# Holding the unshifted term of a VectorE batch until all four tiles are there, in a list-scheduled attention kernel

## The chip, the cores and the metric

One Trainium2 chip, one core, one launch. Times are device microseconds (us) of an execution. Most figures are medians of three to nine executions; a span is that of one profiled execution, from its first instruction to its last, and is some 1.7 us shorter than the time of the same execution. A ratio is the mean time of one kernel's fast runs over that of the other's in the same rounds on the same chip, so it is not quite the ratio of the medians quoted.

## The reference, cut to what matters

Four blocks in a row on x of shape 1 x 2048 x 512: attention, linear attention, attention, linear attention. The attention block has 32 heads of 16 columns that share one K and one V.

```python
def _A_ref(x, wq, wk, wv, wo):           # H = 32, Dh = 16, S = 2048
    q = (x @ wq).reshape(B, S, H, Dh).transpose(0, 2, 1, 3)
    k, v = x @ wk, x @ wv
    p = softmax(einsum("bhqd,bkd->bhqk", q, k) * Dh ** -0.5)
    o = einsum("bhqk,bkd->bhqd", p, v)
    return o.transpose(0, 2, 1, 3).reshape(B, S, H * Dh) @ wo
x = x + _A_ref(_layernorm(x), ...)       # layer 0
x = x + _B_ref(_layernorm(x), ...)       # linear attention, no softmax
x = x + _A_ref(_layernorm(x), ...)       # layer 1
x = x + _B_ref(_layernorm(x), ...)
```

The two softmaxes over 32 x 2048 x 2048 scores are most of the work.

## The kernel before

The program is not written in order. A list scheduler runs while the kernel is built: it has an operation's readiness, a modelled duration and a priority for each engine, and fixes the order of every engine's instructions. What the chip then does is that order, with semaphores.

The scores of both layers are cut into 4096 tiles of 128 x 512. ScalarE exponentiates two or three tiles in one instruction. The other tiles go to VectorE, four to a batch: an integer multiply and add writes a bit pattern that reads as a rough power of two (the unshifted term, P1), three copies with shifted exponents are added to it, and TensorE sums the four terms with four weighted copies of V. So a VectorE tile needs four value matmuls, a ScalarE tile one.

```python
# dstep: one score tile for VectorE; four make a batch
o = add(PE, PASS, lambda e: self.smm(e, [p], db), ..., name="sD", pk=("S", ...))
o = add(DV, tdv(512), lambda e: e.tensor_scalar(out=PTD[:, hp.idx, i * 512:(i + 1) * 512], in0=bank(db),
        scalar1=SCALE * LOG2E * 128.0, scalar2=TOFF, op0=ALU.mult, op1=ALU.add), ..., name="P1")
c["p1"].append(o)
# ... (cut)
# dpass: the terms of a batch; dep[i] is tile i's P1 for r == 0, the shift's one instruction otherwise
for r in range(NTERM):
    dep, src = c["p1"], hp
    split = r == NTERM - 1 and m == 4 and self.npx < NPX and bool(p_ptd.free)
    if split:                       # last term: four pieces on GpSimd
        dep, src = self.pieces(c, m, r, done)
    elif r:                         # one 128x2048 shift on VectorE
        dep, src = self.shift(c, m, r, done)
    for i, p in enumerate(c["pos"]):
        pv = self.add_pv(p, ..., src, dep[0 if r and not split else i], r, 1)
# ... (cut)
# add_pv: a value matmul uses one of TensorE's four column groups
return e.matmul(ps[32 * c:32 * c + 32, 7 * 512:8 * 512], lhsT=Vaug[:, kt, r, :], rhs=..., ...)
# ... (cut)
# Sched._try: a port-sharing VectorE operation does not start while GpSimd is at work
if e == DV and o.port and self.tfree[PO] > self.now + 1e-9 or e == PO and self.dport > self.now + 1e-9:
    continue
```

Some thirty constants steer the scheduler (priorities, how far VectorE may run ahead, how many value matmuls are worth a change of mode). A table, PLAN, changes them every 6 us of modelled time.

The softmax here doesn't subtract the row's maximum and nothing guards it: scores larger than these inputs give would overflow.

## Time and profile before

| | |
|---|---|
| time | 1495.28 us median of 3 (1494.65 to 1497.23) |
| span of the profiled execution | 1497.1 us (its time was 1498.80 us) |
| ScalarE tiles | 2954, in 598 instructions of three and 580 of two |
| VectorE tiles | 1142 |
| ScalarE, sum of service times (see the prediction) | 1420 us |

The groups and the busy line of this profile stand in the prediction. In a group, the figure after the bar is the busy time and the mean ns of one instruction, then the idle time of that engine just before such instructions and what ended it.

### The profile page before, as it was taken

The numbers are of one execution on the slowest core, as the hardware profiler recorded it, in microseconds if no ns is written. First come the engines' busy times: TensorE is split into PE (matmuls) and PEld (weight loads), VectorE is DVE, ScalarE is ACT, GpSimd is POOL, SyncE is SP. The second block draws the span as 40 slices with busy tenths as digits, with TensorE's granted clock in tenths as the row PEclk, the third lists the DMA queues.
The fourth block names the chain that finished last, engine by engine and source line by source line (L and its number), as shares of the span: only waits on it lengthen the run. The fifth ranks groups of instructions, "written<-read, shape, count | busy, mean of one in ns | idle before, by whom it ended". The sixth has DMA issues, their size and how long they took to land.

```text
span 1497.1 us, 38261 instructions
## 1 busy us (share of the span) xinstructions
PE 1459.2 (97%) x16245; PEld 492.0 (33%) x16255; DVE 1376.5 (92%) x2433; ACT 1444.9 (97%) x1426; POOL 853.2 (57%) x1360
## 2 busy tenths in 40 slices
PE   7999999999999999999899999999999999999998
PEld 4322333322333333333442333333333232333334
DVE  7999998999988999899798999989999899989987
ACT  7999999999999999999698999999999999999996
POOL 3556656565563655565544556566565456565654
PEclk9999999999999999999998999999999999999999
DMA  3000000000000000000000000000000000000001
GB/s 118 26 9 5 9 12 5 5 5 4 14 6 7 5 5 17 9 8 9 2 1 5 5 9 8 9 5 5 5 5 15 6 5 5 9 16 8 6 9 57
DMA packets 46251, 17.71 MB, mean 12 GB/s; under 512 B 39936, under 2 KB 45568, under 8 KB 46080
## 3 DMA queue, kind: packets, MB, share of 16 engines
q1 hardware_dynamic: 46080, 15.27, 4.3%
q8 instruction: 127, 2.08, 0.6%
q14 instruction: 44, 0.36, 0.1%
HBM read 5.28 MB, written 2.10 MB: 5 GB/s over the span
## 4 chain that ended last, share of the span: by engine, by line
PE 58%; ACT 23%; DVE 19%; issue 1%; POOL 0%; DMA 0%; SPq 0%; ACTq 0%
PE ps_all L1072 24%; PE ps_all L1035 23%; ACT PTA L1192 20%; DVE PTD L1252 10%; PE ps_all L768 7%; DVE PTD L1323 5%; PE ps_all L772 2%; PE ps_all L1093 2%; DVE Eo L1084 1%; DVE stats L840 1%; ACT e_buf L1576 1%; ACT e_buf L1439 1%; ACT e_buf L1577 1%; DVE e_buf L1446 0%; DVE x_sb L1431 0%
## 5 line engine op out<-in xcount | busy, mean ns | idle before, releaser
L1192 ACT ACTIVATE PTA<-ps_all 128x1536 bf16<-128x1536 f32 (+1 forms) x1178 | 1357.8, 1292 | 18.7 <-PE ps_all L1035 15.0
L1313 POOL TENSOR_SCALAR PTD<-PTD 128x512 uint16<-128x512 uint16 x1124 | 683.2, 618 | 489.2 <-DVE PTD L1323 317.6
L1252 DVE TENSOR_SCALAR PTD<-ps_all 128x512 uint16<-128x512 f32 x1142 | 751.1, 680 | 69.9 <-PE ps_all L1035 65.4
L1035 PE MATMUL ps_all<-QT,Kr 32*128 32x512 bf16 x4141 | 658.6, 385 | 9.9 <-ACT PTA L1192 3.6
L1072 PE MATMUL ps_all<-PTD,Vaug 128*32 128x512 bf16 x4568 | 616.2, 386 | 5.8 <-DVE Eo L1084 5.2
L1072 PE MATMUL ps_all<-PTA,Vaug 128*32 128x512 bf16 x2954 | 533.8, 387 | 0.2
L1323 DVE TENSOR_SCALAR PTD<-PTD 128x2048 uint16<-128x2048 uint16 x577 | 403.6, 711 | 2.2
L1035 PEld LDWEIGHTS ps_all<-QT,Kr 32*128 32x128 bf16 x4141 | 169.1, 91 | 493.0 <-ACT PTA L1192 220.1
L1072 PEld LDWEIGHTS ps_all<-PTD,Vaug 128*32 128x32 bf16 x4568 | 158.6, 94 | 218.1 <-issue 141.5
L1072 PEld LDWEIGHTS ps_all<-PTA,Vaug 128*32 128x32 bf16 x2954 | 131.8, 94 | 145.8 <-issue 114.2
L768 PE MATMUL ps_all<-wqkv_sb,xnT 128*32 128x512 bf16 x960 | 72.5, 382 | 0.1
L1448 POOL TENSOR_SCALAR e_buf<-e_buf 128x512 f32<-128x512 f32 x60 | 36.8, 613 | 43.1 <-ACT e_buf L1439 23.9
L1446 DVE TENSOR_SCALAR e_buf<-ps_all 128x512 f32<-128x512 f32 x60 | 40.9, 685 | 14.3 <-ACT e_buf L1439 14.2
L1439 ACT ACTIVATE e_buf<-ps_all 128x512 f32<-128x512 f32 x64 | 41.7, 655 | 9.7 <-PE ps_all L772 6.5
L1450 POOL TENSOR_TENSOR pqT<-e_buf 128x512 bf16<-128x512 f32 x30 | 38.0, 1268 | 11.8 <-DVE PTD L1323 8.0
L1450 POOL TENSOR_TENSOR pk_tok<-e_buf 128x512 bf16<-128x512 f32 x30 | 38.1, 1272 | 10.5 <-DVE PTD L1323 9.4
L1084 DVE COPY Eo<-ps_all 128x512 f32<-128x512 f32 x62 | 42.3, 682 | 1.5 <-PE ps_all L1072 1.3
L840 DVE BATCH_NORM_STATS2 stats<-x_sb 128x6 f32<-128x512 bf16 x64 | 42.9, 678 | 0.5 <-DMA x_sb<-in_A_x_dram 0.2
L1093 PE MATMUL ps_all<-identf,Eo 128*128 128x128 f32 x256 | 42.4, 289 | 0.0
L768 PE MATMUL ps_all<-wo_sb,OT 128*32 128x512 bf16 x480 | 37.7, 382 | 0.0
L1578 POOL TENSOR_TENSOR pqT<-pqT,e_buf 128x512 bf16<-128x512 bf16 x20 | 23.2, 1164 | 25.1 <-ACT e_buf L1577 6.5
L929 POOL TENSOR_SCALAR Vaug<-Vaug 128x32 bf16<-128x32 bf16 x48 | 14.9, 311 | 32.1 <-DVE Vaug L925 15.5
(102 smaller groups left out, 686.2 us busy)
## 6 DMA issues: line engine op xcount, KB each, us to landing
out_dram<-x_sb SPq DMA_DIRECT2D x16, 128.0 KB, 1.7
OT<-Osb SPq DMA_TRANSPOSE x120, 2.4
xnT<-xn_buf SPq DMA_TRANSPOSE x120, 2.3
wqkv_sb<-in_B_wqkv_dram SPq DMA_DIRECT2D x4, 384.0 KB, 3.1
x_sb<-in_A_x_dram SPq DMA_DIRECT2D x3, 256.0 KB, 3.4
x_sb<-in_A_x_dram SPq DMA_DIRECT2D x1, 768.0 KB, 7.9
wq_sb<-in_A_wq_dram SPq DMA_DIRECT2D x1, 512.0 KB, 6.4
x_sb<-in_A_x_dram SPq DMA_DIRECT2D x1, 512.0 KB, 8.7
```

The source lines that it names most:

```text
L768: i = e.matmul(out[32 * c:32 * c + 32], lhsT=lhsT[:, 32 * c:32 * c + 32], rhs=rhs, start=start, stop=stop, skip_group_check=True)
L840: add(DV, tdv(512), lambda e: e.bn_stats(stats[:, t, 0:6], x_sb[:, t, :]), reads=[("x", t)], writes=[("st", t)], prio=prio, name="bn")
L1035: x = e.matmul(bank(b0 + k), lhsT=Kr[r, m, kt * P:(kt + 1) * P], rhs=QT[r, self.units[u][0] % 2, gs, q0:q0 + n], start=True, stop=True)
L1072: return e.matmul(ps[32 * c:32 * c + 32, 7 * 512:8 * 512], lhsT=Vaug[:, kt, r, :], rhs=src() if callable(src) else src, start=opened[0], s ...
L1084: return (e.copy if oe.eng == AC else e.tensor_copy)(Eo[:, he.idx, :], bank(7))
L1093: i = e.transpose(bank(ht.idx, P, qs * P), Eo[:, he.idx, qs * P:(qs + 1) * P], identf[:])
L1192: oe = add(AC, tac(m * 512), lambda e: e.activation(PTA[:, hp.idx, 0:m * 512], bank(SETS[s][0], m * 512), ACTF.Exp, scale=SCALE), deps=[o] ...
L1252: o = add(DV, tdv(512), lambda e: e.tensor_scalar(out=PTD[:, hp.idx, i * 512:(i + 1) * 512], in0=bank(db), scalar1=SCALE * LOG2E * 128.0, ...
L1313: return e.tensor_scalar(out=PTD[:, ht.idx, i * 512:(i + 1) * 512], in0=PTD[:, hp.idx, i * 512:(i + 1) * 512], scalar1=float(SHIFT[r]), sc ...
L1323: return e.tensor_scalar(out=PTD[:, ht.idx, 0:512 * m], in0=PTD[:, hp.idx, 0:512 * m], scalar1=float(SHIFT[r]), op0=ALU.add, **kw)
L1439: o1 = add(AC, tac(512), lambda e: e.activation(e_buf[:, he.idx, :], bank(h.idx), ACTF.Exp), deps=[o], uses=[h], acq=[he] if fast else [he ...
L1450: add(PO, PHS, lambda e: e.tensor_tensor(out=dst, in0=sh(e_buf[:, hr.idx, :]), in1=sh(e_buf[:, he.idx, :]), op=ALU.add), deps=[o2, o3], us ...
```

## The change

Its intent: VectorE's tiles become ready one after the other, and a value matmul that goes alone uses one of four column groups, so the unshifted term is to wait until its four matmuls can go side by side. With it come a rule for the port that VectorE and GpSimd share, and a new table.

```diff
+PBL = 0.04
+R0 = 1
 PLAN = (
-    (0.0, {... 'NT0': 3, 'DMIN': 1, ... 'MF': 0.285, ... 'PX': 2.788, ...}),
+    (0.0, {... 'NT0': 5, 'DMIN': 2, ... 'MF': 0.413, ... 'PX': 0.523, ...}),
     ... (nearly every row is another)
-            if e == DV and o.port and self.tfree[PO] > self.now + 1e-9 or ...:
+            if e == DV and o.port and self.tfree[PO] > 0.0 and self.tfree[PO] + PBL > self.now + 1e-9 or ...:
                 continue
     ... (cut)
+        if e == PO:
+            self.at(end + PBL, None)
     ... (cut)
-    pv = self.add_pv(p, ..., src, dep[0 if r and not split else i], r, 1)
+    pv = self.add_pv(p, ..., src, c["p1"][-1] if R0 and not r else dep[0 if r and not split else i], r, 1)
```

## The prediction

> **What bounds the kernel now.** I read the page from the top: busy times, slices, chain, groups.
>
> ```profile
> PE 1459.2 (97%) x16245; PEld 492.0 (33%) x16255; DVE 1376.5 (92%) x2433; ACT 1444.9 (97%) x1426; POOL 853.2 (57%) x1360
> ...
> PE 58%; ACT 23%; DVE 19%; issue 1%; POOL 0%; DMA 0%; SPq 0%; ACTq 0%
> ...
> L1192 ACT ACTIVATE PTA<-ps_all 128x1536 bf16<-128x1536 f32 (+1 forms) x1178 | 1357.8, 1292 | 18.7 <-PE ps_all L1035 15.0
> L1313 POOL TENSOR_SCALAR PTD<-PTD 128x512 uint16<-128x512 uint16 x1124 | 683.2, 618 | 489.2 <-DVE PTD L1323 317.6
> L1252 DVE TENSOR_SCALAR PTD<-ps_all 128x512 uint16<-128x512 f32 x1142 | 751.1, 680 | 69.9 <-PE ps_all L1035 65.4
> L1035 PE MATMUL ps_all<-QT,Kr 32*128 32x512 bf16 x4141 | 658.6, 385 | 9.9 <-ACT PTA L1192 3.6
> L1072 PE MATMUL ps_all<-PTD,Vaug 128*32 128x512 bf16 x4568 | 616.2, 386 | 5.8 <-DVE Eo L1084 5.2
> ```
>
> Three engines look nearly full, so busy shares do not name the bound. The first and third groups show how the work is dealt: 4096 score tiles of 512 columns, of which ScalarE exponentiates 2954 in 1178 instructions (598 of three tiles, 580 of two) and VectorE 1142, one each. Every VectorE tile gets four terms, so 4 x 1142 = 4568 value matmuls.
>
> I then looked at single instructions, in time order, in a steady stretch.
>
> ```profile
> 699.07 12.32 ACT L1192 ACTIVATE PTA<-ps_all 128x1024 bf16<-128x1024 f32 x11
> ...
> 705.26 0.39 PE L1072 MATMUL ps_all<-PTD,Vaug 128*32 128x512 bf16 x4
> ...
> 706.33 0.10 PEld L1072 LDWEIGHTS ps_all<-PTD,Vaug 128*32 128x32 bf16 x2 [0.23 <-issue]
> ...
> 706.56 0.59 PE L1072 MATMUL ps_all<-PTD,Vaug 128*32 128x512 bf16 x5
> ```
>
> ScalarE runs eleven exponentials (both sizes; the row prints the first one's) with no gap. TensorE's four value matmuls take 0.39 us together and five take 0.59 us: one round of four column groups costs some 0.2 us more, and 0.39 is mostly the pipe's length. TensorE's 97% is therefore not its throughput; ScalarE's nearly is.
>
> To size that I used the records' start times. A three-tile exponential is followed by the next start after 1331 ns (median), a two-tile one after 904 ns, though they last 1482 and 1067. Taking for every ScalarE form the tenth percentile of its start-to-start times as its service gives 1420 us of service, of which 598 x 1.331 + 580 x 0.904 = 1320 us is the exponentials. From first to last instruction ScalarE spans 1490 us, so it loses about 70 us; 7 us of the span lie outside. The same sum for VectorE gives 1305 us of service and 188 us lost. **ScalarE bounds the kernel**, VectorE has slack. ScalarE's losses by stretch: about 11 us in the first 40 us of feeding and layer norm, some 14 us at the layer change (700 to 800), 7 us near the end (1440 to 1480), and in the steady part 16 us (100 to 680) and 22 us (800 to 1400).
>
> Of the last, one piece stands out; the windows of it:
>
> ```profile
> 812.00:815.00 3.00, 2.52 (x20) 0.45 (x16) 2.49 (x4) 1.59 (x3) 1.13 (x2) 0.67 0.01 3
> 815.00:818.00 3.00, 3.00 (x20) 1.09 (x20) 1.82 (x4) 1.70 (x2) 0.03 (x1) 0.50 0.00 0
> 818.00:822.00 4.00, 4.00 (x27) 0.51 (x23) 2.65 (x5) 2.48 (x2) 1.80 (x3) 0.50 0.13 25
> 822.00:826.00 4.00, 4.00 (x31) 0.82 (x28) 2.51 (x4) 2.48 (x2) 1.88 (x4) 0.50 0.05 8
> ```
>
> The columns are busy time on TensorE, weight load, VectorE, ScalarE and GpSimd, then the granted clock. From 813.0 us TensorE ran 13.7 us at half clock, ScalarE fell to 1.6 to 2.5 us in each window, and its longest steady waits stand here: 1.57, 1.70, 0.60, 1.04 and 1.47 us, together 6.4 us. It is the only dip in the run.
>
> **What the Trainium skill says.** "Perfetto Trace Analysis", section "Identifying the Most-Contended Engine", says that TensorE's matmul busy share is no good measure and that occupancy is fair for Scalar and Vector; the trace agrees, as the rounds above show. The same page, "DVE / Act Engine Instruction", says that a record ends at the write's acknowledgement while the next may begin earlier; the trace agrees: 1482 ns long, 1331 ns apart. "TensorEngine Tiling (Array Packing)", section "Key Properties", says that a change of tiling mode drains TensorE; the 0.23 us ahead of the first weight load after such a change fits. "SBUF — State Buffer", section "SBUF: two separate sides", says that a VectorE two-port operation and a GpSimd one exclude each other for a whole instruction. The trace fits: GpSimd's pieces waited 317.6 us for VectorE's shifts (L1323); and of these shifts a quarter are followed within 601 ns, but the median by 647 ns.
>
> **The change part by part.** There are three, and the program is laid out at build by a list scheduler, so I compared the instruction order of both builds.
>
> 1. The unshifted term's four value matmuls become ready with the last of the four tiles, not each with its own. It removes no instruction. Counted in the built orders: before, the 1142 unshifted matmuls stand in 784 unbroken runs, 546 of a single one and 33 of four; after, 1139 stand in 679 runs, 412 single and 64 of four. So quartets get commoner, but other value matmuls of equal priority still come between. In rounds of 512 columns (in each stretch of one mode, the fullest tile group under in-order issue) the value-type stretches take 2744 before and 2811 after, score stretches 1776 and 1729, full-array work 438 and 425: 4958 against 4965 in all. Without the filler matmuls (four narrow or one wide make a round; 39 rounds before, 36 after) it is 4919 against 4929. Stretches of one mode, so drains, go from 2483 to 2515: 32 x 0.23 = 7 us more. **TensorE is given no less to do**, and it is not the bound.
>
> 2. The scheduler now counts 40 ns after a GpSimd operation before it lets VectorE start a port-sharing one. The roughly 50 ns (647 less 597) on half of 574 shifts is 14 us of VectorE time that the old schedule did not know of. Knowing it cannot remove much, but keeps the order nearer to what the chip does. It lies on VectorE, beside ScalarE's work; its worth is a few us of fewer late tiles.
>
> 3. The table of scheduler constants is new in nearly all of its 6 us steps. By the order it leaves the work almost alone. ScalarE: one more three-tile exponential (+1.33 us), three more key evictions (3 x 0.36), one more projected-matrix and one more value copy, one query copy less, one more mask product: together +2.9 us. VectorE: 3 tiles less (3 x 0.60), 6 shifts less (6 x 0.60), ten query products moved to GpSimd (10 x 0.65): about -12 us. GpSimd: +12 pieces x 0.60, +10 products x 1.13, four phi passes less: about +11 us at 57% busy. Neither is on the path.
>
> Sum for the bound: 1420 + 3 = 1423 us of ScalarE service. What can move is the 70 us of loss. Startup, layer change and end (some 32 us) keep their instructions: 53 rows after the last exponential instead of 51, and 66 between two exponentials at the layer change instead of 63. The steady loss without the dip is 38 - 6 = 32 us; I choose that the better-tracked schedule takes a fifth of it, -6 us. The dip I give an even chance of being gone: -3 us. In all 1495.3 + 3 - 6 - 3 = **1489 us**.
>
> **The rivals.**
> - Packing was the hidden bound: full quartets end ScalarE's waits for score matmuls. For it: those waits are all on TensorE (L1035). Against it: rounds are not fewer. At best the steady 32 us go: near 1465 us.
> - A new wait in place of the old: TensorE works in order, and a late last tile now holds all four matmuls and everything behind them, while the raw buffer stays held. For it: VectorE's start-to-start times scatter. Against it: the shifted terms waited for that last tile anyway, and VectorE got only 3 tiles fewer. It would cost 5 to 15 us: 1500 to 1510 us.
> - The clock: no dip 1489 less 3, two dips 1489 plus 10. Filler matmuls change from 44 narrow and 28 wide to 84 and 15, so the duty around the layer change is another; I can't tell which way.
> - Nothing: the loss is the same and only the work differs, 1498 us.
>
> **Range and chances.** The first case at half effect gives 1477, the second at its low end 1501. Faster by 2% is 1465 us and needs nearly all steady loss gone; slower by 2% is 1525 us, ten times the added work. I give 4%, 93% and 3%.
>
> **What would show it.** Right: ScalarE's exponentials stay at 1331 and 904 ns apart, its service is near 1423 us, its wait for L1035 falls from 15.0 us by a few us, L1252's wait for L1035 stays in the tens, and no group changes its mean. Shift starts at 647 ns should become fewer. The prediction is wrong if the wait of TensorE's weight loads for L1252 or GpSimd grows and ScalarE's wait with it (second rival), if ScalarE's steady loss falls under 15 us (first), or if the clock row shows another number of dips.

## The result, and the profile after

The changed kernel took 1498.66 us (median of 4, 1498.50 to 1498.71) beside 1496.26 us (4 runs): ratio 1.0017, interval 1.0000 to 1.0034. Five more rounds (after_again, below) gave 1.0015, interval 1.0002 to 1.0029. It is the same by the 2% measure, and a trace slower, where 0.4% faster had been forecast.

The busy line, the chain by engine and the groups of the changed kernel, to be held against those in the prediction (L1192 is now L1196, L1313 L1317, L1252 L1256, L1035 L1039, L1072 L1076):

```profile
PE 1458.3 (97%) x16282; PEld 491.5 (33%) x16282; DVE 1362.2 (91%) x2413; ACT 1446.9 (97%) x1432; POOL 862.9 (58%) x1374
...
PE 53%; ACT 38%; DVE 7%; POOL 1%; issue 1%; DMA 0%; POOLq 0%
...
L1196 ACT ACTIVATE PTA<-ps_all 128x1024 bf16<-128x1024 f32 (+1 forms) x1179 | 1356.8, 1297 | 13.9 <-PE ps_all L1039 10.5
L1317 POOL TENSOR_SCALAR PTD<-PTD 128x512 uint16<-128x512 uint16 x1136 | 690.7, 617 | 502.8 <-DVE PTD L1327 341.0
L1256 DVE TENSOR_SCALAR PTD<-ps_all 128x512 uint16<-128x512 f32 x1139 | 752.1, 681 | 75.7 <-PE ps_all L1039 70.4
L1039 PE MATMUL ps_all<-QT,Kr 32*128 32x512 bf16 x4150 | 639.7, 383 | 13.8 <-ACT PTA L1196 8.1
L1076 PE MATMUL ps_all<-PTD,Vaug 128*32 128x512 bf16 x4556 | 622.2, 384 | 3.6 <-DVE Eo L1088 3.0
```

In the lines shown, no count and no mean moved by more than 1.1%. The trace has one spell at half clock, of 3.4 us at 726 us, where the one before had 13.7 us at 813 us. ScalarE's wait for score matmuls seems to have fallen, from 15.0 to 10.5 us, just as forecast; the next section shows that this is the clock and not the change. The busy times of VectorE, ScalarE and TensorE are the old ones within 1.1%.

### The profile page after: what moved, and what is told of

It is laid out like the page before. It is cut to its first block, busy times and chain, and to the rows that moved or that the text cites. A ratio compares the mean times of both kernels' runs of the same rounds, so it can differ in the third digit from the quotient of the medians.

```text
span 1496.8 us, 38319 instructions
## 1 busy us (share of the span) xinstructions
PE 1458.3 (97%) x16282; PEld 491.5 (33%) x16282; DVE 1362.2 (91%) x2413; ACT 1446.9 (97%) x1432; POOL 862.9 (58%) x1374
## 4 chain that ended last, share of the span: by engine, by line
PE 53%; ACT 38%; DVE 7%; POOL 1%; issue 1%; DMA 0%; POOLq 0%
ACT PTA L1196 35%; PE ps_all L1076 22%; PE ps_all L1039 20%; PE ps_all L772 6%; DVE PTD L1256 3%; PE ps_all L776 2%; PE ps_all L1097 2%; DVE PTD L1327 1%; ACT e_buf L1443 1%; DVE stats L844 1%; POOL pqT L1582 1%; ACT e_buf L1580 1%; ACT e_buf L1581 1%; DVE Eo L1088 0%; DVE e_buf L1450 0%
## 5 line engine op out<-in xcount | busy, mean ns | idle before, releaser
L1196 ACT ACTIVATE PTA<-ps_all 128x1024 bf16<-128x1024 f32 (+1 forms) x1179 | 1356.8, 1297 | 13.9 <-PE ps_all L1039 10.5
L1317 POOL TENSOR_SCALAR PTD<-PTD 128x512 uint16<-128x512 uint16 x1136 | 690.7, 617 | 502.8 <-DVE PTD L1327 341.0
L1256 DVE TENSOR_SCALAR PTD<-ps_all 128x512 uint16<-128x512 f32 x1139 | 752.1, 681 | 75.7 <-PE ps_all L1039 70.4
L1039 PE MATMUL ps_all<-QT,Kr 32*128 32x512 bf16 x4150 | 639.7, 383 | 13.8 <-ACT PTA L1196 8.1
L1076 PE MATMUL ps_all<-PTD,Vaug 128*32 128x512 bf16 x4556 | 622.2, 384 | 3.6 <-DVE Eo L1088 3.0
L1076 PE MATMUL ps_all<-PTA,Vaug 128*32 128x512 bf16 x2957 | 543.5, 386 | 0.0
L1327 DVE TENSOR_SCALAR PTD<-PTD 128x2048 uint16<-128x2048 uint16 x571 | 393.7, 703 | 1.6
L1039 PEld LDWEIGHTS ps_all<-QT,Kr 32*128 32x128 bf16 x4150 | 165.0, 91 | 485.8 <-ACT PTA L1196 234.8
L1076 PEld LDWEIGHTS ps_all<-PTD,Vaug 128*32 128x32 bf16 x4556 | 159.1, 94 | 218.3 <-issue 141.9
L1076 PEld LDWEIGHTS ps_all<-PTA,Vaug 128*32 128x32 bf16 x2957 | 134.2, 94 | 147.7 <-issue 106.5
L1582 POOL TENSOR_TENSOR pqT<-pqT,e_buf 128x512 bf16<-128x512 bf16 x30 | 34.3, 1163 | 26.6 <-ACT e_buf L1581 20.3
L776 PE MATMUL ps_all<-Msb,pqT 128*128 128x512 bf16 x128 | 32.5, 379 | 0.9
```

Source lines behind the costliest of these rows:

```text
L776: return e.matmul(out, lhsT=lhsT, rhs=rhs, start=start, stop=stop, skip_group_check=True)
L1039: x = e.matmul(bank(b0 + k), lhsT=Kr[r, m, kt * P:(kt + 1) * P], rhs=QT[r, self.units[u][0] % 2, gs, q0:q0 + n], start=True, stop=True)
L1196: oe = add(AC, tac(m * 512), lambda e: e.activation(PTA[:, hp.idx, 0:m * 512], bank(SETS[s][0], m * 512), ACTF.Exp, scale=SCALE), deps=[o] ...
L1317: return e.tensor_scalar(out=PTD[:, ht.idx, i * 512:(i + 1) * 512], in0=PTD[:, hp.idx, i * 512:(i + 1) * 512], scalar1=float(SHIFT[r]), sc ...
L1327: return e.tensor_scalar(out=PTD[:, ht.idx, 0:512 * m], in0=PTD[:, hp.idx, 0:512 * m], scalar1=float(SHIFT[r]), op0=ALU.add, **kw)
```

## The experiments

Eighteen kernels ran. My theory at the start was that ScalarE alone bounds the kernel, that packing is worth nothing, and that the new table takes a few us of ScalarE's losses. The rivals were that TensorE's packing bounds after all, and that the three parts have large effects that cancel.

A first build tells something before any run: the old table with the wait for four tiles added does not build. The scheduler ends with value matmuls that never became ready. A table belongs to its rule more closely than I had thought. (With both rules the old table does build; that kernel was not run.)

### The same kernels once more

before_again is the text of the changed kernel with all three parts undone; the order of every engine is the kernel before's to the instruction.

```diff
-PBL = 0.04            -R0 = 1            -PLAN = (new table)
+PBL = 0.0             +R0 = 0            +PLAN = (old table)
```

> The changed kernel's text with all three parts undone (no wait for all four tiles, no 40 ns, the old table): the built order equals the kernel before in every instruction, so this is a second look at the kernel before. Theory (the clock spell belongs to the old order): 1494 to 1498 us, and its trace shows the one half-clock spell near 813 us again, of some 14 us. Rival (the spell is chance): no spell or one elsewhere, and a span up to 6 us shorter than 1497 us.

It took 1495.29 us, in a run of four that held one of 1505.96 us at a lower mean clock (0.990). Its trace has a span of 1492.4 us, and no spell at half clock near 813 us, only one of 3.4 us at 1467 us. The rival held. The same windows as in the prediction, of before_again:

```profile
812.00:815.00 3.00, 2.52 (x28) 0.99 (x30) 3.00 (x6) 2.11 (x2) 0.97 (x2) 1.00 0.01 3
815.00:818.00 3.00, 3.00 (x35) 0.66 (x30) 3.00 (x8) 3.00 (x4) 1.16 (x2) 1.00 0.06 11
818.00:822.00 4.00, 4.00 (x48) 1.17 (x46) 4.00 (x7) 4.00 (x5) 2.74 (x6) 1.00 0.13 25
822.00:826.00 4.00, 4.00 (x49) 1.15 (x45) 4.00 (x8) 3.86 (x4) 2.74 (x5) 1.00 0.02 4
```

From 815 us on ScalarE (the fourth busy figure) and VectorE (the third) are full or nearly so here, where they stood idle for a third of the time or more in the trace of before. One and the same order has the spell in one execution and not in the next; with it the span is 4.7 us longer. The first trace was no typical execution: the 38 later executions of the kernel before, on four chips, have medians of 1494.5 to 1495.5 us by chip and round, with single ones up to 1505.94; 36 of them have a mean clock of 0.997 or more, where the traced one had 0.995. ScalarE's wait for score matmuls is 10.2 us in this trace,

```profile
L1196 ACT ACTIVATE PTA<-ps_all 128x1536 bf16<-128x1536 f32 (+1 forms) x1178 | 1357.5, 1295 | 13.8 <-PE ps_all L1039 10.2
```

so there is no fall from 15.0 to 10.5 us where the old order runs without that spell.

after_again is the changed kernel with a blank line added.

> The changed kernel again (a blank line added), five rounds beside the kernel before. Theory (no gain, a little longer round the layer change): 1497 to 1500 us, 1.001 to 1.004 of the kernel before with an interval that leaves out 0.996. Rival (my predicted 0.996 was missed by chance in few runs): ratio under 0.999.

It took 1497.38 us (five runs, 1497.34 to 1498.68) beside 1495.40 us of nine, ratio 1.0015 (1.0002 to 1.0029); no spell in its trace, span 1495.6 us. Its order and before_again's can be compared with little of the clock in the way. I sum ScalarE's services as in the prediction (1331 and 904 ns for the exponentials of both, the tenth percentile of its own start-to-start times for every other form) and call the rest between first and last instruction lost. "Start" is up to 60 us past the first exponential, "change" from 10 us before the last one of layer 0 to 80 us past the first of layer 1, "end" the last 10 us of exponentials and all behind; flat_both, with both rules and no table, comes below.

| us | before_again | after_again | flat_both |
|---|---|---|---|
| span | 1492.4 | 1495.6 | 1555.3 |
| ScalarE's service | 1419.4 | 1420.7 | 1436.9 |
| lost at the start | 7.5 | 6.5 | 8.1 |
| lost in the steady parts | 34.1 | 33.7 | 64.9 |
| lost at the layer change | 15.9 | 17.6 | 23.2 |
| lost at the end | 8.0 | 9.1 | 14.2 |
| outside ScalarE's first and last | 7.4 | 7.9 | 7.8 |
| at half clock | 3.4 | 0.0 | 17.1 |

The steady parts, for which the whole change was made, lose what they lost. The 3.2 us more are 1.3 of service, 1.7 at the layer change, 1.1 at the end, less 1.0 at the start, and some 0.5 outside, within rounding. The 3.4 us at half clock of before_again lie in its end, so the two orders differ there by rather more than 1.1. ScalarE in time order at the layer change, of before_again:

```profile
711.60 1.48 ACT L1196 ACTIVATE PTA<-ps_all 128x1536 bf16<-128x1536 f32 x1
...
717.21 1.09 ACT L1443 ACTIVATE e_buf<-ps_all 128x512 f32<-128x512 f32 x2 [2.83 <-PE ps_all L776]
...
725.02 0.58 ACT L881 COPY xnT<-ps_all 128x512 bf16<-128x512 bf16 x1 [1.43 <-PE ps_all L875]
...
749.52 1.43 ACT L1196 ACTIVATE PTA<-ps_all 128x1536 bf16<-128x1536 f32 x1
```

and of after_again:

```profile
710.00 3.77 ACT L1197 ACTIVATE PTA<-ps_all 128x1536 bf16<-128x1536 f32 x3
...
725.92 0.59 ACT L882 COPY xnT<-ps_all 128x512 bf16<-128x512 bf16 x1 [2.15 <-PE ps_all L876]
...
749.52 1.11 ACT L1581 ACTIVATE e_buf<-ps_all 128x512 f32<-128x512 f32 x2
750.48 1.20 ACT L1582 ACTIVATE e_buf<-e_buf 128x512 f32<-128x512 f32 x2
752.17 1.45 ACT L1197 ACTIVATE PTA<-ps_all 128x1536 bf16<-128x1536 f32 x1 [0.50 <-PE ps_all L1040]
```

Layer 0's exponentials end at 713.1 and 713.8 us, layer 1's begin at 749.5 and 752.2 us: 36.4 us against 38.4 us between them. At 749.5 us, where the old order starts with layer 1, the new one still has two pairs of the linear block's logarithm and exponential to do. So 2 of the 3 us lie in a stretch that the wait for four tiles does not touch; the new table put it so.

The clock can also be taken out of the times. Within one kernel they follow the mean granted clock: the four runs of flat_none (below) took 1548.41 us at 0.999, 1550.70 at 0.997, 1555.49 at 0.993 and 1560.98 at 0.988. One slope fitted to the runs of all eighteen kernels and of the kernel before beside them is 1.29 us for each 0.001, and leaves a scatter of at most 1.4 us (standard deviation) in any of them. Taken to a clock of 1 by this line, which makes them estimates, before_again and the kernel before lie 0.2 us apart, as the same order should, and after_again is 3.9 us slower than the kernel before. (An order may itself draw more or fewer spells; no run here tests that.)

### Which engine holds the time

Three kernels keep the changed kernel's order and take work from one engine. Their outputs are wrong, which doesn't matter for the times. A fourth, thin_both, takes from two.

```diff
 # thin_exp: once a buffer was filled, three-tile exponentials compute 1408 of 1536 columns
-activation(PTA[:, hp.idx, 0:m * 512], bank(SETS[s][0], m * 512), ACTF.Exp, ...)
+activation(PTA[:, hp.idx, 0:w], bank(SETS[s][0], w), ACTF.Exp, ...)          # w = 1408
 # thin_value: all but the first and last value matmuls of an accumulation stream 448 columns
-e.matmul(ps[32 * c:32 * c + 32, 7 * 512:8 * 512], lhsT=..., rhs=src, ...)
+e.matmul(ps[32 * c:32 * c + 32, 7 * 512:7 * 512 + n], lhsT=..., rhs=src[:, 0:n], ...)   # n = 448
 # thin_p1: once a slot was filled, VectorE's P1 computes 460 of 512 columns
-tensor_scalar(out=PTD[:, hp.idx, i * 512:(i + 1) * 512], in0=bank(db), ...)
+tensor_scalar(out=PTD[:, hp.idx, i * 512:i * 512 + w], in0=bank(db, w), ...)            # w = 460
```

> Wrong result on purpose. The changed kernel with its order untouched, but all but the first few three-tile exponentials on ScalarE compute 1408 of 1536 columns: some 594 x 0.107 us = 63 us less ScalarE work. Theory (ScalarE bounds): 1498 less 50 to 63, so 1435 to 1448 us. Rival (TensorE bounds): at most 15 us less.

> Wrong result on purpose. The changed kernel with its order untouched, but all value matmuls except the first and last of an accumulation stream 448 columns instead of 512: rounds fall from 2811 to 2557, some 54 us less TensorE work. Theory (ScalarE bounds): 1490 to 1499 us. Rival (value matmuls and their packing bound): 1445 to 1465 us.

> Wrong result on purpose. The changed kernel with its order untouched, but VectorE's tiles (the eviction that makes the unshifted term) compute 460 of 512 columns once each buffer slot was filled once: some 1090 x 0.054 us = 59 us less VectorE work. Theory (VectorE has slack): 1488 to 1499 us. Rival (VectorE bounds with ScalarE): below 1465 us.

> Wrong result on purpose. The changed kernel, order untouched, with both cuts: three-tile exponentials at 1408 columns and value matmuls at 448. Alone they gave 16 and 9 us. Theory (ScalarE and TensorE are a few us apart, each hides the other's cut): well over the sum, 40 to 60 us less, 1438 to 1458 us. Rival (a third thing, the chain between engines, holds both): 25 us or less, 1473 us or more.

| kernel | work taken away | median us | ratio to before | worth, us |
|---|---|---|---|---|
| thin_exp | 63 us of ScalarE | 1482.96 | 0.9918 | 14.5 |
| thin_value | 54 us of TensorE | 1489.97 | 0.9967 | 7.2 |
| thin_p1 | 59 us of VectorE | 1496.88 | 1.0014 | 0.1 |
| thin_both | 63 of ScalarE and 54 of TensorE | 1466.01 | 0.9807 | 31.1 |

Since the thin kernels and after_again did not run in the same rounds, the worth is taken from the ratios: after_again's 1.0015 less the kernel's, times 1495 us. (The expectation of thin_both counts from 1498.7 us, and so has 16 and 9.) The intervals of the two ratios together leave each worth uncertain by some 3 us; taken to full clock, thin_p1's is 3 us and the others change by less than 2. VectorE's slack came as forecast, and TensorE gave little alone. ScalarE did not behave: less than a quarter of the work taken from it showed up, which is what the rival (TensorE bounds) had expected. My theory of one bound fell here. The chains that ended last, by engine, of thin_exp, thin_value and thin_both:

```profile
PE 70%; DVE 25%; ACT 3%; POOL 1%; issue 0%; DMA 0%; POOLq 0%
```

```profile
ACT 57%; PE 31%; DVE 10%; POOL 1%; issue 1%; DMA 0%; POOLq 0%; SPq 0%
```

```profile
PE 59%; DVE 36%; ACT 3%; POOL 1%; issue 1%; DMA 0%; POOLq 0%; SPq 0%
```

With shorter exponentials ScalarE, which had 38% of the chain in the changed kernel, all but leaves it, and TensorE takes it over. (The chain is one path only: ScalarE's share is 23% in before, 27% in before_again and 38% in after, three kernels of nearly one speed.) The group of the exponentials in thin_exp says the same:

```profile
L1201 ACT ACTIVATE PTA<-ps_all 128x1024 bf16<-128x1024 f32 (+2 forms) x1179 | 1311.8, 1197 | 38.8 <-PE ps_all L1039 30.5
```

Its wait for score matmuls goes from 10.5 to 30.5 us, and its loss by my sum from 67 us (after_again) to 117 us. So my reading is that ScalarE is first, that the work through TensorE stands some 15 us behind, and that the two hide each other's cuts: both together give 31.1 us, more than the 21.7 of the single ones. That is the theory that I put in place of the first, and it is not shown whole: a ScalarE that was plainly first would have left thin_value nothing, and thin_both's 31.1 us lie between the 40 to 60 of the theory and the 25 of its rival. They don't give 54 either. ScalarE still loses 99 us in thin_both, and VectorE has 36% of the chain; a third limit, VectorE or the waits between three engines in a fixed order, is next. Which of the two, no run settles.

For the question at hand this is enough: 254 rounds of value matmuls fewer gave 7 us. The change saves no round at all (2811 against 2744 among value-type stretches), so there is nothing for it to give.

### The two rules without a tuned table

Four kernels use one constant row (the kernel's own default) in place of the table, with neither rule, with one, and with both.

```diff
-PLAN = ( ... some 240 rows ... )
+PLAN = ()            # R0 = 0 or 1, PBL = 0.0 or 0.04
```

> One constant row in place of the table of scheduler constants, neither wait nor 40 ns. Leaves ScalarE 3012 tiles (58 more than the kernel before, 58 x 0.444 = 26 us). Both theories: 1505 to 1530 us. It is the base line for the next three, whose table was tuned for neither rule.

> The constant row with the wait for all four tiles alone. Against the constant row with nothing. Theory (packing is worth nothing: rounds 5108 against 5112): within 6 us of it, from ScalarE's 3018 tiles + 3 us. Rival (filled column groups pay): over 10 us faster than it. Second rival (the later release costs): over 10 us slower.

> The constant row with the 40 ns rule alone. ScalarE gets 3021 tiles, + 4 us against the constant row with nothing. Theory (the rule only makes the schedule truer): within 6 us of it. Rival (it repairs late tiles): over 10 us faster.

> The constant row with both rules. ScalarE gets 3005 tiles, - 3 us. Theory: within 6 us of the constant row with nothing. Rival (the two rules pay only together): over 10 us faster.

They took 1553.10, 1548.44, 1554.23 and 1554.61 us. flat_none is far over its expected 1505 to 1530 us: I had counted only the 26 us of ScalarE tiles. The other three lie within 5 us of it, as expected. One pair can't tell a worth of 5 us from the scatter between two schedules, so I ran two more pairs, with a constant row taken from each table at 120 us.

```diff
-PLAN = ()
+PLAN = ((0.0, {the row that the new (old) table holds at 120 us}),)     # R0 = 0 or 1, PBL = 0.0
```

> One constant row again, now the one that the new table holds at 120 us, without the wait for all four tiles and without the 40 ns. ScalarE keeps 3033 tiles. Base line for the next run; 1520 to 1570 us.

> The same row with the wait for all four tiles alone. Rounds 5069 against 5097, stretches of one mode 2570 against 2624, ScalarE 10 tiles less (- 4 us). Theory (the wait by itself is worth the few us of rounds and drains that it saves, at most 0.5%): 0 to 8 us faster than its base line. Rival (worth nothing): within 2 us. Second rival (filled column groups pay well): over 15 us faster.

> One constant row, the one that the old table holds at 120 us, neither rule. ScalarE keeps 2943 tiles. Base line for the next run; 1500 to 1580 us.

> That row with the wait for all four tiles alone. Rounds 5063 against 5093, stretches 2548 against 2556, ScalarE 6 tiles more (+ 3 us). Theory: 0 to 8 us faster than its base line. Rival (worth nothing): within 2 us or slower. Second rival (filled column groups pay well): over 15 us faster.

| row | without the wait | with it | difference | rounds | stretches of one mode |
|---|---|---|---|---|---|
| the default | 1553.10 | 1548.44 | -4.7 | 5112, 5108 | 2630, 2581 |
| from the new table | 1564.73 | 1565.72 | +1.0 | 5097, 5069 | 2624, 2570 |
| from the old table | 1537.01 | 1534.35 | -2.7 | 5093, 5063 | 2556, 2548 |

The mean is 2 us, the sign changes, and the runs of one kernel spread by up to 12 us (1561.96 to 1574.05 in rowN_none) with their clock (0.995 to 0.987). The second row came as its rival had it, worth nothing, the third as the theory. But the clock was lower with the wait in the second row (mean 0.986 against 0.992); taken to full clock the three differences are -2.2, -7.6 and -5.3 us. A fourth pair, flat_40ns and flat_both, has +0.4 us as measured and +1.2 at full clock. Over the four pairs that is a mean gain of 1.5 us as measured and 3.5 at full clock. The wait may be worth a few us; it is not worth 15. The 40 ns rule made both of its pairs slower, by 1.1 us (flat_none to flat_40ns) and 6.2 us (flat_wait4 to flat_both).

Since the wait alone seldom keeps a quartet together, one more kernel lets the unshifted matmuls go ahead of other value matmuls, which leaves 166 unbroken quartets in the built order where flat_wait4 has 49.

```diff
-prio=2.0 + 1e-4 * u, ...
+prio=(1.99 if wt == 1 and r == 0 else 2.0) + 1e-4 * u, ...
```

> The constant row with the wait for all four tiles, and the four unshifted value matmuls go ahead of other value matmuls, so that they stand together: 166 unbroken quartets where the wait alone leaves 49, and 386 runs for 635. But rounds are 5144 for 5108 and stretches of one mode 2627 for 2581. Theory (what counts is rounds and drains, not quartets): 1548 to 1562 us, not faster than the wait alone (1548.4). Rival (whole quartets pay): under 1540 us.

It took 1555.43 us, 7 us more than flat_wait4. Its rounds (5144) and stretches (2627) are more. Whole quartets are not what counts. That the other value matmuls get broken up in their stead is my reading of the counts; no run shows it by itself.

### The rules under a table that was tuned for the other

```diff
 new_nowait4: -R0 = 1        +R0 = 0        (new table, 40 ns kept)
 new_no40ns:  -PBL = 0.04    +PBL = 0.0     (new table, wait kept)
 old_40ns:    -PBL = 0.0     +PBL = 0.04    (old table, no wait)
```

> The changed kernel with the wait for all four tiles undone, its table kept. Rounds 5113 against 4965, ScalarE 2 tiles more. Theory (a table fits only the order it was tuned in, the rule itself is worth nothing): 1515 to 1550 us. Rival (the rule is worth something by itself): this, but then the constant row with the wait should have gained as much, and it gained 5 us. Second rival (the table is general): 1495 to 1503 us.

> The changed kernel with the 40 ns rule undone, its table kept. ScalarE gets 24 tiles more (+ 11 us), rounds 5075. Theory (the table fits only its own order): 1515 to 1550 us. Rival (the table is general): 1500 to 1510 us.

> The kernel before with the 40 ns rule alone, its old table kept. ScalarE gets 11 tiles less (- 5 us), rounds 5139, of which 55 fillers. Theory (the table fits only its own order): 1515 to 1550 us. Rival (the table is general and the rule good): 1488 to 1496 us.

They took 1557.34, 1538.77 and 1580.38 us. The first two are 60 and 41 us over the changed kernel, the third 85 us over the kernel before, all in the same rounds (1497.38 and 1495.40 us). new_nowait4 and old_40ns are even beyond my range, and no faster than flat_40ns (1554.23), which has the same rules and no table. Each of these edits would be called a disaster by someone who tried it alone with the table left as it was, and the untuned rows show that the rule itself does nearly nothing. The group of the exponentials in old_40ns shows the way in which a schedule goes bad:

```profile
L1196 ACT ACTIVATE PTA<-ps_all 128x1536 bf16<-128x1536 f32 (+1 forms) x1169 | 1355.6, 1276 | 90.0 <-PE ps_all L1039 87.3
```

VectorE has more tiles (1153) than in the kernel before, so ScalarE has less work, and yet it waits 87.3 us for score matmuls; the span also has six half-clock spells, 34.1 us in all.

What a table is worth follows from flat_both and the changed kernel, which have the same rules: ratios of 1.0395 and 1.0015, so 3.8%, 57 us. For the old rules flat_none's ratio says it directly: 3.9%, 58 us. (At full clock both are 53 us.) In the ledger above, of the 59.7 us between the spans of flat_both and after_again, 16.2 are ScalarE's service (48 tiles that VectorE doesn't take, less a few other evictions) and some 43.6 its losses, 31.2 of them in the steady parts. **The new table wins back under the new rules what the old one had won under the old, and no more.**

No correct version that I ran beats the kernel before.

## Why the prediction was wrong

**The step that failed** is the sum's "-6 us", the claim that "the better-tracked schedule takes a fifth" of 32 us of steady loss. It was a choice, without a row of the profile behind it, and it measured -0.4 us (34.1 to 33.7). Behind it stood part 2's "keeps the order nearer to what the chip does", taken as a gain. What the runs show is that a table is tuned to one order, and that a new rule throws the tuning away first.

**The second failure** is "-3 us" for the dip. The spell is chance: the identical order ran without it. It cost 4.7 us in the one execution that was traced, but the 1495.3 us from which I subtracted was the median of three others (1494.65 to 1497.23), and of the 38 later ones only two had a mean clock as low as that trace's. I took from a median what only the profiled run had paid.

**A cost that was left out**: the startup, the layer change and the end "keep their instructions", so I gave them no difference. Instructions they kept, but not their order; 2 us of the 3 stand there.

**"+3 us" of ScalarE work** was right in sign and measured 1.3 us, in a sum of 1420 whose services scatter by a nanosecond each, about 1 us of the sum, from trace to trace.

**"32 x 0.23 = 7 us"** of drains is too much per drain. In before_again's trace the next round starts 0.216 us (median) after the last one within a mode, and 0.314 us after it across a change of mode (2482 changes; 0.304 at the fifth percentile). So a change of mode costs some 0.10 us, and 32 of them 3 us. The 0.23 us was the gap ahead of the first weight load, not what the change adds.

**What held.** TensorE got no less to do by the counts of the built orders; its busy time is unchanged too, 1459.2 and 1458.3 us, though that is no measure of its work. The exponentials stayed at 1331 and 904 ns apart within 1 ns, VectorE's wait for L1039 stayed in the tens (70.4 us). Fewer shifts are followed only after some 650 ns, as forecast, but hardly: 273 of 574 in before_again, 249 of 568 in after_again (620 to 700 ns counted; the rest of the bulk lies near 600). By an estimate that is 24 x 50 ns = 1 us of VectorE, which thin_p1 shows to be worth next to nothing; that the median falls from 645 to 625 ns only says that it lies between the two kinds. The first rival, packing as a hidden bound, fell with thin_value and flat_quartet. The second, a new wait of TensorE, did not show: its weight loads' wait for VectorE's tiles went from 2.6 to 1.6 us and that for GpSimd from 14.8 to 18.0 us, and ScalarE's from 10.2 to 10.5 us (before_again and after_again). Of the four rivals the last, "Nothing: the loss is the same and only the work differs, 1498 us", is the one that came. Its number is luck in part: it is the work's +3 us on the median, of which 1.3 us were measured, and the loss grew by about as much.

**A line misread.** The prediction takes GpSimd's wait of 317.6 us for the shifts as a sign of the shared port. It is no sign: the scheduler gives every long GpSimd operation a semaphore wait for the VectorE operation ahead of it (`o.deps = o.deps + [self.order[DV][...]]` in `_start`). The spacing of the shifts is one: in before_again 268 of the 273 slow ones began with a GpSimd record still open, which ran for another 0.18 us (median); of the 245 shifts followed within 620 ns 66 did, and theirs ran for 0.07 us.

**"ScalarE bounds the kernel"** was wrong about the distance at the least: 63 us less of it gave 14.5. That ScalarE comes first is the likelier reading (14.5 us of 63, where TensorE gave 7.2 of 54), and not shown.

Open: why exactly the new table orders the layer change as it does, whether the wait's few us over four pairs are real, and what stands behind ScalarE and TensorE in thin_both.

## What to carry to other kernels

When three engines are near full and the order was tuned as a whole, ask of a local improvement first whether it lowers the count that it is meant to lower (here rounds and drains, both of which can be read from the built order, and neither fell in the changed kernel); if not, it has little to give, and a retuned table only returns to where it was. Judge a rule under constants that were tuned for neither side, in more than one pair, since the same edit cost 40 to 85 us under a table made for something else. Hold the mean clock of the runs beside every small difference. And look at a second trace of the kernel before, before a wait in the first one is put on the bill.

## What the Trainium skill lacked or had wrong

- "Perfetto Trace Analysis", section "Identifying the Most-Contended Engine", says to optimize the engine of highest occupancy first. It does not say that the next one may stand so near that the gain stops at once: 63 us taken from ScalarE, at 97% busy, gave 14.5 us, and with 54 us taken from TensorE as well 31.1 us.
- "TensorE: Matmul & The Clock Gate", section "What's actually happening", tells of a free-running activity window of 3413 ns. The traces agree: all spells at half clock but those that begin after the program's last instruction last multiples of 3.4 us (3.4, 6.8, 10.2, 13.7, 17.1, 20.5), and within a trace they start whole multiples of 3.413 us apart. What it lacks is that one and the same order can meet a spell in mid-run in one execution and not in the next: 13.7 us at 813 us in one trace of an order, none there in another, 4.7 us of span apart.
- No page that I found gives a cost for the drain at a change of tiling mode; the start times in before_again's trace give some 0.10 us (0.314 us from round to round across a change, 0.216 us within a mode).
